# Attention and a two-level mixture of experts on one core: six edits to queues, slots and evictions

## The chip, the cores and the metric

The kernel runs on 1 core of one Trainium2 chip. The metric is device time in microseconds for one execution; the time before is 511.01 us, the median of 3 runs (510.89 to 512.64). The core has TensorE (matrix multiply, PE in the profile, with its weight loads as PEld), VectorE (DVE), ScalarE (ACT), GpSimd (POOL) and the sync engine (SP), which mainly issues transfers. Transfers can be issued on the queues of SP, ACT and GpSimd.

## The reference, cut to what matters

```
def _attn_ref(q, k, v):                      # q: 8 x 16 x 384 x 64, k and v: 8 x 1 x 384 x 64
    scores = 1.0 / np.sqrt(64) * np.matmul(q, k.transpose(0, 1, 3, 2))
    attn = softmax(scores)
    return np.matmul(attn, v)

def _moe_ref(x, w_group, w_expert, w1, w2):  # x: 3072 x 1024, 4 groups of 4 experts, F = 1024
    g_idx = argmax(x @ w_group); g_w = its softmax weight
    for each group g, for its tokens:
        e_idx = argmax(xg @ w_expert[g]); e_w = its softmax weight
        out[token] = g_w * e_w * (np.maximum(xg @ w1[g, e], 0.0) @ w2[g, e])
```

The attention output of each token (16 heads of 64) is the token's x of 1024. Every token goes to one of 16 experts.

## The kernel before, in words

Attention runs batch by batch: 8 batches (b) of 3 row tiles of 128 tokens (t = 3b + j), each tile with 8 units (u) of two heads. The order is written out by hand. The main loop (L782) has 96 slots, 12 for each batch; slot i does units 2i and 2i + 1, four slots make a tile, and p is i mod 4. In each slot TensorE makes the scores (L204) in one of two double banks of PSUM, VectorE takes the row maxima (L215), ScalarE the exponentials with their sums (L218), GpSimd the division (L233), and VectorE transposes the result two slots later into a ring (L239). In slots with p of 2 or 3 TensorE multiplies the tile before with v (pv, L255) into the four rotating banks of `ps_x`, which `xbank` hands out in turn. At p = 3 the result goes to x (`pv_out`, L261), as float32 for the gate and as bf16 (`xb`) for the experts.

The first batch has its own start: `load_k_first` (L134) loads the keys twice, one copy on SP's queue and one on ACT's, then `load_q` (L102) issues the first queries on both queues. TensorE runs 7 matmuls on a blank tile (`busy`, L97), then transposes the keys (`prep_first`, L142), runs 2 more blank ones, and transposes the queries (`q_group`, L172).

The experts of a batch run one batch later. The table `later` holds calls by slot and place in the slot: "s" after the scores, "b" between the two units' softmax, "m0", "m1" and "m2" around the expert's matmuls, "v" before the ring's transposes, "w" after them, "e" after the division, "g" at the end. `advance(n)` (L702) lets the pending expert issue n groups of three steps; its matmuls fill TensorE in slots with p of 0 or 1.

For each batch the gate works on the first tile's tokens (slot 12b + 8: `logits`, L272; slot 12b + 9: `logits_out`, L285, and `gate_first`, L296). `gate_choose` (L336) counts the choices with a matmul on `ones` into a bank of `ps_x`; `gate_score` (L345) reads the bank on VectorE, and `gate_pick` (L353) gives the index of the most chosen expert. That expert, the batch's main one, is applied to the whole batch with the gate as a scale (zero for the other tokens). `load_main` (L457) reads the index into a register on GpSimd and issues the two weight matrices there as four transfers, cast to bf16 on the way, into two buffers for each matrix. `keep_xb` (L467) stores a batch's bf16 x in a scratch tensor on SP's queue; only the loop at the end (L895), for tokens that the main experts did not cover, reads it.

After the main loop comes the end for the last batch, b = 7. `load_second` (L462) loads the second most chosen expert's weights. `few_ready`, `few_turn`, `few_flags`, `few_places` and `few_gather` (L538 to L650) pick out the few tokens of that expert: their x, gate and row number are gathered by matmuls with a selection matrix. `few_gather` moves gate and row number with a float32 matmul (L643). `main_expert(7)` runs meanwhile. Then `few_expert` (L652) applies the second expert to the gathered tokens: hidden layer in two banks (L662), each evicted half by ScalarE and half by VectorE (L670, L672), output in two banks (L678), each again in two halves (L684, L685), and a scatter to the output rows by an indirect transfer on GpSimd (L688). The stores of the main expert (`store`, L532) go out on SP's queue.

Of the kernel before, what the change touches and what calls it, by code (L numbers as in the profile page):

```python
# [11 lines left out]
I32 = mybir.dt.int32  # L12
P = 128
# [6 lines left out]
def kernel(  # L20
# [113 lines left out]
    def load_k_first():  # L134
        kk = qpool.tile([P, NB * D], FP32, tag="kk", bufs=1)
        kk = kk[:, 0:2 * ST * D].rearrange("p (j t d) -> p j t d", j=ST, t=2)
        kv = k[0, 0].rearrange("(p j) d -> p j d", j=ST)
        nc.sync.dma_start(out=kk[:, :, 0, :], in_=kv)
        nc.scalar.dma_start(out=kk[:, :, 1, :], in_=kv)
        st["kk", 0] = kk  # L140
# [397 lines left out]
    def few_ready():  # L538
# [4 lines left out]
        for name, t, widths in (  # L543
            ("16", c16, (("eye", P), ("tri", P), ("sel", ST * P), ("f", 4), ("cum", 4))),
            ("32", c32, (
                ("cols", P), ("tri", P), ("sel", ST * P), ("prod", ST * GE), ("ohs", GE), ("rows", 2 * ST), ("pos", 4),
                ("f", ST), ("fits", 1), ("gate", 1), ("low", 1), ("at", 1),
            )),
        ):
            at_ = 0  # L550
            for part, w in widths:
                fw[part + name] = t[:, at_:at_ + w]
                at_ += w
# [12 lines left out]
        rows = fw["rows32"].rearrange("p (j t) -> p j t", t=2)[:, :, 1]  # L566
# [7 lines left out]
        )  # L574
        fw["xt"] = [ppool.tile([P, Dm], BF16, tag="pr", name="xtok") for _ in range(ST)]
# [48 lines left out]
    def few_gather():  # L624
        fw = st["few"]
        rows = fw["rows32"].rearrange("p (j t) -> p j t", t=2)
        nc.vector.tensor_copy(out=rows[:, :, 0], in_=st["gsel", B - 1][1][:])
# [14 lines left out]
        for j in range(ST):  # L642
            nc.tensor.matmul(  # L643
                out=bank[:, 0:2], lhsT=fw["sel32"][:, ts(j, P)], rhs=rows[:, j, :], start=(j == 0), stop=(j == ST - 1)
            )
        nc.vector.tensor_copy(out=fw["gate32"], in_=bank[:, 0:1])
        nc.vector.tensor_scalar(
            out=fw["at32"].bitcast(I32), in0=bank[:, 1:2], scalar1=fw["fits32"], scalar2=float(NR), op0=ALU.mult,
# [3 lines left out]
    def few_expert():  # L652
# [5 lines left out]
        for half in range(2):  # L658
# [7 lines left out]
            for e in range(2):  # L666
                h = h_t[:, 4 * half + 2 * e:4 * half + 2 * e + 2, 0:P]
                hp = bank[:, ts(e, 2 * P)].rearrange("p (k t) -> p k t", k=2)
                if e:
                    nc.vector.tensor_scalar(out=h, in0=hp, scalar1=0.0, scalar2=None, op0=ALU.max)  # L670
                else:
                    nc.scalar.activation(out=h, in_=hp, func=ACTF.Relu)  # L672
        ys = [bank_end() for _ in range(2)]
        y = pool.tile([P, Dm], FP32, tag="y", name="few_y", bufs=3)
        for part in range(2):
            for nh in range(2):
# [5 lines left out]
                if part:  # L682
                    a, m, z = 512 * nh, 512 * nh + 256, 512 * (nh + 1)
                    nc.scalar.activation(out=y[:, a:m], in_=ys[nh][:, 0:256], func=ACTF.Copy, scale=gate)  # L684
                    nc.vector.tensor_scalar(  # L685
                        out=y[:, m:z], in0=ys[nh][:, 256:512], scalar1=gate, scalar2=None, op0=ALU.mult
                    )
        nc.gpsimd.indirect_dma_start(  # L688
# [34 lines left out]
    for b in range(B):  # L723
        s0 = SB * b
        for x, j0, j1 in ((s0 + 8, 0, 1), (s0 + 16, 1, ST)):
            at(x, "m2", logits, b, j0, j1)
            at(x + 1, "v", logits_out, b, j0, j1)
        at(s0 + 9, "v", gate_first, b)
        at(s0 + 9, "m2", gate_choose, b)
        at(s0 + 9, "w", gate_score, b)  # L730
        at(s0 + 9, "w", gate_pick, b)
        at(s0 + (13 if b == B - 1 else 12), "w", gate_picked, b)
        at(s0 + 9, "g", load_main, b, 0)
        at(s0 + (10 if b == B - 1 else 9), "g", load_main, b, 1)
        at(s0 + 16, "g", keep_xb, b)
# [46 lines left out]
    for i in range(NSL):  # L782
# [8 lines left out]
        if p < 2:  # L791
# [3 lines left out]
            advance(2 if p == 1 and t % ST > 0 else 1)  # L795
# [36 lines left out]
    run(i + 4, "g")  # L832
# [58 lines left out]
    advance(1000)  # L891
    few_expert()
# [53 lines left out]
```

## Time and profile before

| what | value |
|---|---|
| median of 3 runs | 511.01 us (510.89 to 512.64) |
| the profiled execution | 513.33 us |
| its span, first to last instruction | 511.9 us |
| TensorE busy / its weight loads | 486.9 / 262.6 us |
| VectorE / ScalarE / GpSimd busy | 414.0 / 322.3 / 288.4 us |
| mean granted TensorE clock | 0.991 |
| bytes moved by DMA | 84.14 MB, mean 164 GB/s |

The profile is of one execution. Rows in order of time give the start, the duration, the engine (with q for its queue's issue work), the line, the operation, the tiles and the count of merged instructions; in brackets stands the idle time of the engine before it and what ended it. "issue" means that the engine waited for nothing that the profile shows. A row of a line's statistics has the least, median and largest duration in ns and the first and last start in us. A row of transfers has the tiles, the queue, the count, the size of one and the median time from issue to landing.

### The profile page before, as it was taken

The page shows a single profiled execution, that of the slowest core. Times are in us where ns is not written, and L with a number is a line of the kernel's source. Part 1 is how long each engine was busy: PE and PEld are TensorE (multiplying, and loading weights), DVE is VectorE, ACT ScalarE, POOL GpSimd, SP SyncE. Part 2 cuts the span into 40 slices and gives each one's busy share as a digit, 9 for nine tenths or more (in the row PEclk, how much of TensorE's full clock was granted, in tenths as well). Part 3 has the DMA queues.
Part 4 walks back from the last instruction along what each step waited for, and adds up shares of the span by engine and source line. Part 5 has one row for each costly group of instructions (what it writes and reads, how often), then busy time and mean ns, then how long its engine had stood idle before and what let it go on. Part 6 is the DMA issues. An engine that isn't in the chain of part 4 may idle for free. (4 is left out here: it accounts for less than half of the span.)

```text
span 511.9 us, 20030 instructions
## 1 busy us (share of the span) xinstructions
PE 486.9 (95%) x8245; PEld 262.6 (51%) x8262; DVE 414.0 (81%) x739; ACT 322.3 (63%) x1002; POOL 288.4 (56%) x518
## 2 busy tenths in 40 slices
PE   7687799999999999999999999999999999999993
PEld 3144355555465455555465455555455455555651
DVE  3899979988789889998799879988899879871621
ACT  3776766676675775676676776676676766652511
POOL 1656855584576654584576654584576664574200
PEclk9799999999999999999999999999999999999998
DMA  8522898379945999389946999389946992089992
GB/s 109 128 45 43 150 238 213 74 144 232 255 97 106 213 249 229 74 142 231 264 91 113 215 245 226 74 148 232 255 94 120 219 231 96 3 149 246 260 239 86
DMA packets 65180, 84.14 MB, mean 164 GB/s; under 512 B 21163, under 2 KB 40619, under 8 KB 65088
## 3 DMA queue, kind: packets, MB, share of 16 engines
q0 software_dynamic: 19152, 37.84, 40.9%
q1 hardware_dynamic: 44448, 44.65, 35.0%
q8 instruction: 66, 1.08, 0.8%
q10 hardware_dynamic: 1488, 0.36, 0.4%
q14 instruction: 26, 0.21, 0.1%
HBM read 101.61 MB, written 19.40 MB: 236 GB/s over the span
## 5 line engine op out<-in xcount | busy, mean ns | idle before, releaser
L233 POOL TENSOR_SCALAR pr<-pr,rinv 128x384 f32<-128x384 f32 x384 | 218.3, 589 | 153.5 <-DVE rinv L229 140.5
L218 ACT ACTIVATE pr<-s,nmx 128x384 f32<-128x384 f32 x384 | 218.0, 579 | 132.9 <-DVE nmx L215 119.4
L215 DVE TENSOR_REDUCE nmx<-s 128x2 f32<-128x768 f32 x192 | 174.4, 948 | 45.8 <-PE s L204 44.8
L239 DVE STREAM_TRANSPOSE ring<-pr 128x768 f32<-128x768 f32 x192 | 175.2, 951 | 0.0
L204 PE MATMUL s<-kt,qt 64*64 64x384 f32 x1536 | 151.9, 505 | 12.3 <-ACT pr L218 10.2
L255 PE MATMUL x<-ring,v_sb 32*64 32x256 f32 x4608 | 138.1, 378 | 0.2 <-issue 0.2
L255 PEld LDWEIGHTS x<-ring,v_sb 32*64 32x64 f32 x4608 | 101.8, 131 | 43.2 <-issue 23.5
L204 PEld LDWEIGHTS s<-kt,qt 64*64 64x64 f32 x1536 | 48.0, 133 | 83.6 <-ACT pr L218 43.9
L218 ACT ACTIVATION_READ_ACCUMULATOR pr<-s,nmx 128x1 f32 x384 | 77.9, 203 | 0.0
L477 PE MATMUL x<-xb,w 128*128 128x384 bf16 x448 | 76.5, 327 | 0.0
L477 PEld LDWEIGHTS <-w 128*128 128x128 bf16 x512 | 48.2, 98 | 42.6 <-issue 12.6
L491 PE MATMUL x<-w,h_t 128*128 128x512 bf16 x276 | 64.6, 380 | 0.6
L491 PEld LDWEIGHTS <-h_t 128*128 128x128 bf16 x384 | 35.8, 98 | 52.0 <-issue 11.9
L452 POOL DMA_DIRECT2D w<-in_moe_w_dram x36 | 27.9, 784 | 6.0 <-PE sb L491 4.3
L269 ACT COPY xt<-x 128x256 f32<-128x256 f32 x96 | 28.8, 386 | 3.2 <-PE x L255 2.9
L483 ACT ACTIVATE h_t<-x 128x384 bf16<-128x384 f32 x56 | 25.4, 503 | 5.9 <-PE x L477 3.1
L270 POOL CAST xb<-xt 128x1024 bf16<-128x1024 f32 x24 | 25.0, 1040 | 4.6 <-ACT xt L269 4.6
L509 ACT ACTIVATE y<-x,gsel 128x512 f32<-128x512 f32 x36 | 25.0, 693 | 3.3 <-PE x L491 3.3
L193 DVE STREAM_TRANSPOSE qt<-q_sb 128x512 f32<-128x512 f32 x38 | 26.1, 687 | 0.0
L491 PE MATMUL sb<-w,h_t 128*128 128x512 bf16 x92 | 21.2, 379 | 0.2
L509 ACT ACTIVATE y<-sb,gsel 128x512 f32<-128x512 f32 x9 | 6.2, 688 | 16.8 <-PE sb L491 16.8
L229 DVE RECIPROCAL rinv<-ssum 128x4 f32<-128x4 f32 x96 | 13.8, 143 | 3.1 <-ACT pr L218 3.1
(126 smaller groups left out, 168.3 us busy)
## 6 DMA issues: line engine op xcount, KB each, us to landing
w<-in_moe_w_dram POOLq DMA_DIRECT2D x36, 1024.0 KB, 19.7
q_sb<-in_q_dram SPq DMA_DIRECT2D x76, 224.0 KB, 6.3
out_dram<-y SPq DMA_DIRECT2D x96, 128.0 KB, 6.3
xb_scratch<-xb SPq DMA_DIRECT2D x8, 768.0 KB, 4.3
v_sb<-in_v_dram SPq DMA_DIRECT2D x32, 96.0 KB, 3.7
kk<-in_k_dram SPq DMA_DIRECT2D x28, 92.0 KB, 4.2
q_sb<-in_q_dram SPq DMA_DIRECT2D x16, 128.0 KB, 3.4
q_sb<-in_q_dram ACTq DMA_DIRECT2D x4, 64.0 KB, 3.3
```

The source lines that it names most:

```text
L193: nc.vector.transpose(out=qt[:].rearrange("p (x d) -> p x d", d=32), in_=q_sb[:, :, 0:32])
L204: nc.tensor.matmul(out=s[m * D:(m + 1) * D, h, 0:S], lhsT=qt[r, ts(2 * cc + m, D)], rhs=kt[r, :], start=True, stop=True, tile_position=(h ...
L215: nc.vector.tensor_reduce(out=nmx[:], in_=s[:, :, 0:S], axis=AX.X, op=ALU.max, negate=True)
L218: nc.scalar.activation(out=pr[:, h, :], in_=s[:, h, 0:S], func=ACTF.Exp, bias=nmx[:, h:h + 1], scale=1.0, accum_out=ssum[:, k, h:h + 1],)
L233: nc.gpsimd.tensor_scalar(out=pr, in0=pr, scalar1=rinv[:, k, h:h + 1], scalar2=1.0, op0=ALU.mult, op1=ALU.mult)
L239: nc.vector.transpose(out=ring[:, (u // 4) % 3, u % 4].rearrange("p h s -> p (h s)"), in_=st.pop(("pr", u))[:].rearrange("p h s -> p (h s)"),)
L255: nc.tensor.matmul(out=o[i][h * D:(h + 1) * D, 0:2 * P].rearrange("d (g c q) -> d g c q", g=2, c=4), lhsT=v_sb[r, n, :], rhs=ring[r, a:z + ...
L269: nc.scalar.copy(out=xt[:, :, ts(i, 32)], in_=o[:, 0:2 * P].rearrange("p (c q) -> p c q", c=KO))
L452: nc.gpsimd.dma_start(out=w[:, o:o + 4, :], in_=(w1f, w2f)[n][ds(e, 1), :, o:o + 4, :].rearrange("o p c f -> (o p) c f"))
L477: nc.tensor.matmul(out=hp[:, 0:S], lhsT=w1[:, ko, ts(fc, P)], rhs=xb[:, ko, :], start=(ko == 0), stop=(ko == KO - 1))
L491: nc.tensor.matmul(out=yp, lhsT=h_t[:, fo, ts(j, P)], rhs=w2[:, fo, ts(nh, 512)], start=(fo == 0), stop=(fo == FO - 1),)
L509: nc.scalar.activation(out=y[:, ts(nh, 512)], in_=yp, func=ACTF.Copy, scale=g)
```

## The change

Six edits, all in the order of work or in small tiles:

1. The two copies of the first keys are issued on GpSimd's queue, after the identity is made and before `wge` is cleared.
2. Batch 0's count is issued in slot 10, after that slot's scores, its score between the two units' softmax, and the pick and the weights' load at the end of that slot. In the other batches the count stays in slot 12b + 9 but stands one `advance(1)` earlier, at a new place "m3" between the last two groups. The transpose of the first logits and `gate_first` move from "v" to "m0", which leaves VectorE's order as it was.
3. The last batch's main weights are issued at "w", before the slot's division on GpSimd, instead of at "g", behind it.
4. The last batch's bf16 x is kept (`keep_xb`) after the last store of the main expert, instead of before that expert begins.
5. In `few_expert` each bank is evicted by one engine: the first by ScalarE, the second by VectorE.
6. In `few_gather` gate and row number are split into bf16 parts (three and two), moved with a bf16 matmul and added up again.

```diff
@@ load_k_first
-        nc.sync.dma_start(out=kk[:, :, 0, :], in_=kv)
-        nc.scalar.dma_start(out=kk[:, :, 1, :], in_=kv)
+        for t in range(2):
+            nc.gpsimd.dma_start(out=kk[:, :, t, :], in_=kv)
@@ few_ready
-            ("16", c16, (("eye", P), ("tri", P), ("sel", ST * P), ("f", 4), ("cum", 4))),
+            ("16", c16, (("eye", P), ("tri", P), ("sel", ST * P), ("f", 4), ("cum", 4), ("parts", 5 * ST))),
...
+        nc.gpsimd.tensor_copy(out=parts[:, :, 3], in_=rows)
+        nc.gpsimd.tensor_tensor(out=parts[:, :, 4], in0=rows, in1=parts[:, :, 3], op=ALU.subtract)
@@ few_gather
-        rows = fw["rows32"].rearrange("p (j t) -> p j t", t=2)
-        nc.vector.tensor_copy(out=rows[:, :, 0], in_=st["gsel", B - 1][1][:])
+        parts, rest = fw["parts16"].rearrange("p (j t) -> p j t", t=5), fw["rest32"]
+        gsel = st["gsel", B - 1][1][:]
+        nc.vector.tensor_copy(out=parts[:, :, 0], in_=gsel)
+        nc.vector.tensor_tensor(out=rest, in0=gsel, in1=parts[:, :, 0], op=ALU.subtract)
+        nc.vector.tensor_copy(out=parts[:, :, 1], in_=rest)
+        nc.vector.tensor_tensor(out=parts[:, :, 2], in0=rest, in1=parts[:, :, 1], op=ALU.subtract)
...
-                out=bank[:, 0:2], lhsT=fw["sel32"][:, ts(j, P)], rhs=rows[:, j, :], start=(j == 0), stop=(j == ST - 1)
+                out=bank[:, 0:5], lhsT=fw["sel16"][:, ts(j, P)], rhs=parts[:, j, :], start=(j == 0), stop=(j == ST - 1)
             )
-        nc.vector.tensor_copy(out=fw["gate32"], in_=bank[:, 0:1])
+        nc.vector.tensor_reduce(out=fw["gate32"], in_=bank[:, 0:3], axis=AX.X, op=ALU.add)
+        nc.vector.tensor_reduce(out=fw["row32"], in_=bank[:, 3:5], axis=AX.X, op=ALU.add)
@@ few_expert
-            for e in range(2):
...
+            h, hp = h_t[:, 4 * half:4 * half + 4, 0:P], bank.rearrange("p (k t) -> p k t", k=4)
+            if half:
+                nc.vector.tensor_scalar(out=h, in0=hp, scalar1=0.0, scalar2=None, op0=ALU.max)
+            else:
+                nc.scalar.activation(out=h, in_=hp, func=ACTF.Relu)
...
+                if part and nh:
                     nc.vector.tensor_scalar(
-                        out=y[:, m:z], in0=ys[nh][:, 256:512], scalar1=gate, scalar2=None, op0=ALU.mult
+                        out=y[:, ts(nh, 512)], in0=ys[nh], scalar1=gate, scalar2=None, op0=ALU.mult
                     )
+                elif part:
+                    nc.scalar.activation(out=y[:, ts(nh, 512)], in_=ys[nh], func=ACTF.Copy, scale=gate)
@@ the table of calls
-            at(x + 1, "v", logits_out, b, j0, j1)
-        at(s0 + 9, "v", gate_first, b)
-        at(s0 + 9, "m2", gate_choose, b)
-        at(s0 + 9, "w", gate_score, b)
-        at(s0 + 9, "w", gate_pick, b)
+            at(x + 1, "v" if j0 else "m0", logits_out, b, j0, j1)
+        at(s0 + 9, "m0", gate_first, b)
+        at(s0 + (9 if b else 10), "m3" if b else "s", gate_choose, b)
+        at(s0 + (9 if b else 10), "w" if b else "b", gate_score, b)
+        at(s0 + (9 if b else 10), "w", gate_pick, b)
         at(s0 + (13 if b == B - 1 else 12), "w", gate_picked, b)
-        at(s0 + 9, "g", load_main, b, 0)
-        at(s0 + (10 if b == B - 1 else 9), "g", load_main, b, 1)
-        at(s0 + 16, "g", keep_xb, b)
+        if b == B - 1:
+            at(s0 + 9, "w", load_main, b, 0)
+            at(s0 + 10, "w", load_main, b, 1)
+        else:
+            at(s0 + (9 if b else 10), "g", load_main, b, 0)
+            at(s0 + (9 if b else 10), "g", load_main, b, 1)
+            at(s0 + 16, "g", keep_xb, b)
@@ the main loop
-            advance(2 if p == 1 and t % ST > 0 else 1)
+            advance(1)
+            run(i, "m3")
+            if p == 1 and t % ST > 0:
+                advance(1)
@@ the end
-    run(i + 4, "g")
...
     advance(1000)
+    keep_xb(b)
     few_expert()
```

More of the change, by code (lines that the diff above doesn't have):

```diff
@@ L564, in few_ready @@
         nc.gpsimd.memset(c16[:, 2 * P + ST * P:2 * P + ST * P + 8], 0.0)
-        rows = fw["rows32"].rearrange("p (j t) -> p j t", t=2)[:, :, 1]
+        rows, parts = fw["rows32"], fw["parts16"].rearrange("p (j t) -> p j t", t=5)
         nc.gpsimd.iota(
```

13 lines of the change are left out of this document (2 added, 11 removed).

## The prediction

> **What bounds the kernel now.** I read the page's busy shares and slices first, then busy time by stretch, who waited for whom on TensorE, and the order of time at the three places that the change touches.
>
> ```profile
> 300.00:400.00 100.00, 99.79 (x1775) 53.93 (x1764) 88.75 (x152) 68.09 (x218) 63.06 (x110) 1.00 0.79 172
> ```
>
> After the stretch's bounds, the columns are the length, the busy time of TensorE, its weight loads, VectorE, ScalarE and GpSimd (with counts), the granted clock, the DMA share and GB/s. TensorE has no free time here (99.79 of 100 us, clock 1.00), and the same holds from some 60 us to 500 us. Work moved between other engines there is worth nothing; only TensorE work, or a wait of TensorE, is. What remains is the start, batch 0 (no expert work beside it yet), and the last 10 us.
>
> Times add up against the profiled execution (513.33 us, span 511.9, so 1.4 us lie around it). It is 2.3 us above the median 511.01; I carry differences over to the median. The runs shown spread over 1.7 us, so I take 0.5% (2.55 us) as what a measurement of this kernel tells from no change.
>
> **First keys.** The start in order of time, and the landing times:
>
> ```profile
> 1.08 0.68 SPq L138 DMA_DIRECT2D kk<-in_k_dram  x1
> 1.35 0.29 POOL masks.py:199 TENSOR_SCALAR_AFFINE_SELECT ident<-ident 128x128 f32<-128x128 f32 x1
> 3.78 0.15 PEld L100 LDWEIGHTS <-blank 128*128 128x128 bf16 x1 [0.28 <-issue]
> 4.29 0.18 PEld L146 LDWEIGHTS x<-ident,kk 128*128 128x128 f32 x1 [0.36 <-issue]
> 5.06 0.36 PEld L100 LDWEIGHTS <-blank 128*128 128x128 bf16 x2
> 6.09 0.72 PEld L181 LDWEIGHTS x<-ident,q_sb 128*128 128x128 f32 x4 [0.67 <-issue]
> ...
> kk<-in_k_dram SPq DMA_DIRECT2D x1, 96.0 KB, 3.1
> kk<-in_k_dram ACTq DMA_DIRECT2D x1, 96.0 KB, 2.6
> ```
>
> The keys land at 1.08 + 3.1 = 4.18, just as the seven blank matmuls run out (one load each 0.43 us, so the next slot is 4.21), and their transposes begin at 4.29. The two blanks after them would end at 5.06 + 0.86 = 5.92 and the queries' transposes start at 6.09: the keys have 0.17 us of slack, and nothing could start more than that sooner. All later work hangs on this chain.
>
> After the change both halves go out on GpSimd's queue, behind the identity (1.35 + 0.29 = 1.64). SP's and ACT's query issues move up by one key issue (0.68 us); nothing waits for that, because TensorE takes the keys first. What a GpSimd issue costs is seen on the weights only:
>
> ```profile
> 52.22 3.25 POOL L452 DMA_DIRECT2D w<-in_moe_w_dram  x4 [1.64 <-issue]
> L452 POOL DMA_DIRECT2D w<-in_moe_w_dram x36: 750/770/990, 52.2 to 472.0; - x36
> issue: 1.6, 1
> DMA to landing us min/median/max: 8.3/8.3/8.3
> 56.00:57.00 1.00, 1.00 (x15) 0.41 (x4) 0.91 (x2) 0.42 (x2) 1.00 (x3) 1.00 1.10 199
> ```
>
> The first GpSimd issue of the program stood 1.64 us with nothing to wait for and then took 0.99 us; of the other 35 none stood so, and the median is 0.77. I read it as a cost of the first use. The keys become that first use: 1.64 + 1.64 = 3.28, first issue done 4.27, second lands 2.6 us later (ACT's row, the same 96 KB) at 6.87. That is 2.6 us after 4.29, less 0.17 of slack: **+2.4**. Lower end: no first-use cost, 1.64 + 0.77 + 2.6 = 5.0, +0.5; or below it nothing late at all, −0.2 with the slack. Upper end: the first weight half landed 8.3 us after its issue; 1.05 MB at the 199 GB/s of that stretch are 5.3, which leaves 3.0, and 96 KB add 0.5: 4.27 + 3.5 = 7.8, +3.3. I take 2.6 as the landing since its row has the same size. The identity's cover is no help: it ends before either issue could.
>
> The Trainium skill (DMA: Bandwidth & Descriptors, Specifications) puts the first byte at about 1 µs on GpSimd's path and 0.6 µs on SP's and ACT's, which alone would make the keys some 0.4 us later beside the later issue. The rows above carry a larger and one-off delay; the page has none for it, and the sum goes by the rows.
>
> **Batch 0's count.** Slots 9 to 12 in order of time:
>
> ```profile
> 45.66 1.83 DVE L239 STREAM_TRANSPOSE ring<-pr 128x768 f32<-128x768 f32 x2
> 45.79 0.17 PE L339 MATMUL x<-first,ones 128*128 128x16 bf16 x1 [1.81 <-DVE first L304]
> 45.89 0.21 PEld L204 LDWEIGHTS s<-kt,qt 64*64 64x64 f32 x8 [2.08 <-ACT pr L218]
> 47.41 0.14 DVE L348 SCALAR_TENSOR_TENSOR scr<-x,tie 128x16 f32<-128x16 f32 x1
> 47.54 2.41 PEld L255 LDWEIGHTS x<-ring,v_sb 32*64 32x64 f32 x96 [0.70 <-DVE scr L348]
> 48.13 1.79 DVE L215 TENSOR_REDUCE nmx<-s 128x2 f32<-128x768 f32 x2
> 50.44 0.88 PE L204 MATMUL s<-kt,qt 64*64 64x384 f32 x8
> 51.64 1.82 DVE L215 TENSOR_REDUCE nmx<-s 128x2 f32<-128x768 f32 x2
> 55.14 1.52 PE L204 MATMUL s<-kt,qt 64*64 64x384 f32 x16
> 56.09 1.82 DVE L215 TENSOR_REDUCE nmx<-s 128x2 f32<-128x768 f32 x2 [0.82 <-PE s L204]
> ```
>
> The count's 1.81 us stall of TensorE goes: slot 10's scores load some 0.5 us sooner. But VectorE has no gap from 45.66 to 53.4, and its work is only reordered. What is late next is the bank: pv takes four rotating banks, the last of them the count's, so it waits for L348 (0.70 in the row). After the change L348 stands behind slot 10's first reduce: 47.41 + reciprocal 0.1 + reduce 0.91 + 0.14 = 48.6 instead of 47.55. So pv starts 1.06 later, ends at 51.5 (2.85 long), and the next scores, behind it on TensorE, go from 50.44 to 51.5. Their reduce follows 0.95 later (55.14 to 56.09), at 52.45 instead of 51.64: 0.8 later. I take **+0.5**, since slot 10's exponentials, some 0.5 us sooner, can give part of it back. Ends: −0.5 (only the stall counts) and +1.1 (pv's whole delay). Batch 0's weights are issued a step later, some 4 us; the experts need them 20 us after, and the normalisations behind that issue on GpSimd are read two slots later, so both are covered; if not, batch 0's first expert would wait.
>
> For the other batches the count moves up by one eighth of an expert's first half:
>
> ```profile
> 441.33 4.08 PE L477 MATMUL x<-xb,w 128*128 128x384 bf16 x24
> 443.22 0.18 DVE L304 TENSOR_TENSOR first<-oh 128x16 bf16<-128x16 f32 x1
> 445.24 0.17 PE L339 MATMUL x<-first,ones 128*128 128x16 bf16 x1
> 446.41 2.28 POOL L233 TENSOR_SCALAR pr<-pr,rinv 128x384 f32<-128x384 f32 x4 [4.44 <-DVE rinv L229]
> 448.63 1.58 POOL L452 DMA_DIRECT2D w<-in_moe_w_dram  x2
> ```
>
> L339 comes 4.08/3 = 1.36 sooner, at 443.9; its input is ready at 443.4. Covered by 0.5 us, so nothing; were the cover gone, seven batches would pay the lateness. The last batch's weights pass four normalisations, 2.2 us sooner, and these come 1.6 us later, two slots ahead of their readers: nothing.
>
> **The end.**
>
> ```profile
> xb_scratch<-xb SPq DMA_DIRECT2D x1, 768.0 KB, 9.8
> 500.00:501.00 1.00, 0.88 (x5) 0.33 (x4) 0.42 (x1) 0.38 (x1) 0.00 (x0) 1.00 1.09 375
> 502.51 1.89 PE L678 MATMUL sb<-w,few_h 128*128 128x512 bf16 x8 [0.52 <-DMA w<-in_moe_w_dram]
> 504.43 0.47 ACT L684 ACTIVATE few_y<-sb,c 128x256 f32<-128x256 f32 x1 [0.39 <-PE sb L678]
> 504.94 0.48 DVE L685 TENSOR_SCALAR few_y<-sb,c 128x256 f32<-128x256 f32 x1 [0.38 <-ACT few_y L684]
> 505.72 1.12 POOL L688 DMA_INDIRECT out_dram<-few_y,c  x1 [22.35 <-DVE few_y L685]
> 490.40 8.94 SPq L534 DMA_DIRECT2D out_dram<-y  x12
> L511 DVE TENSOR_SCALAR y<-sb,gsel 128x512 f32<-128x512 f32 x3 | 2.3, 751 | 7.7 <-PE sb L491 4.4 <-PE x L879 3.3
> ```
>
> DMA is full to 501, and TensorE waits 0.52 for the last weights. The 768 KB of x leave their way (some 3 us of transfer at about 250 GB/s), and the weights start sooner: the 0.52 goes. The two halves of the last bank ran one behind the other, 504.43 to 505.42 = 0.99; one engine takes 0.75: 0.24 goes. **−0.8**; ends −0.2 (weights still late) and −1.0. On SP x is issued behind the last store, at 499.4; with the landing of 9.8 us it is there by 509.2, about when the scattered rows are, so it costs nothing, or 0.5 if slower. The hidden-layer evictions are merged too, but TensorE reaches their readers later.
>
> ```profile
> 485.19 0.83 PE L643 MATMUL x<-c 128*128 128x2 f32 x6
> 485.88 3.61 PE L491 MATMUL sb<-w,h_t 128*128 128x512 bf16 x15
> ```
>
> Gates in parts: three more small VectorE operations (0.14 for one, by L348's row) make the input ready at 485.19 + 0.45 = 485.6; three single-pass matmuls instead of six passes are done at about 486.0, where L491 began at 485.88: **+0.1** (−0.3 to +0.5). GpSimd's two added operations fall into idle time.
>
> **Sum:** 2.4 + 0.5 − 0.8 + 0.1 = +2.2. 511.01 + 2.2 = **513.2** (profiled: 515.5).
>
> **Rivals.**
>
> 1. *The clock* (slower). TensorE then sits empty from 4.84 until the keys come. After a sparse stretch in the kernel before, the clock fell:
>
> ```profile
> 18.00:19.00 1.00, 1.00 (x12) 0.30 (x8) 0.97 (x3) 0.54 (x2) 0.06 (x1) 0.50 1.03 230
> ```
>
> At 0.50 eight score matmuls take about 1.3 instead of 0.88 us, 0.4 for each of the first three slots: +1.2, 514.4, and up to 515.3 with the late landing (+0.9). For it speaks that the dip is there already; against it that the same dip may only move. It decides once the keys are over 2 us late. The Trainium skill (TensorE: Matmul & The Clock Gate) gives two clocks, half when idle for a window of about 3.4 µs and full after one busy; by that the gap falls short of a window but can spoil the first one.
>
> 2. *No first-use cost*: keys at 5.0, start +0.5 instead of +2.4, so 511.3. For it: the stall is one event. Against: nothing else explains it.
>
> 3. *Everything hides and gains* (faster): start −0.2, batch 0 −0.5, end −1.0, gates −0.3, and the clock dip of 17 to 25 us falls elsewhere, −0.8: −2.8, 508.2. Against it: keys issued later must land as soon.
>
> 4. *The weights are late all the same*, held by their own queue: the end gives −0.2, 513.8.
>
> **How the numbers follow.** Forecast 0.40 (own range 512.2 to 514.2, of it 0.16 above 513.57), rival 1 0.17, rival 2 0.20, rival 3 0.16 (0.01 of it within), rival 4 0.07. Faster 0.15; within 0.5% 0.24 + 0.20 + 0.01 = 0.45; slower 0.16 + 0.17 + 0.07 = 0.40. The range 509.3 to 515.0 leaves out the ends of rivals 3 and 1.
>
> **What would show it.** Keys' transposes at about 6.9, GpSimd idle ahead of its first key issue; L348 behind the first reduce of slot 10 and pv 1 us later; no DMA wait at the last matmuls. Keys before 5 us, or pv no later, would make me wrong.

## The result, and the profile after

The changed kernel took 515.91 us, the median of 6 runs (514.21 to 516.32), beside 511.7 us for the kernel before on the same chip (6 runs, 510.89 to 512.64). The ratio is 1.0077, with a 95% interval of 1.0057 to 1.0097. It is slower, by 4.2 us where 2.2 were forecast, and above the top of the range.

The profiled execution of the changed kernel took 516.11 us (span 514.6), that of the kernel before 513.33 (span 511.9). The two differ by 2.8 us only, because the profiled execution of before was 1.6 us above its median. So the experiments below are compared by medians, and traces by places in the program.

The start of the changed kernel in order of time (columns as before):

```profile
1.84 1.71 POOL L139 DMA_DIRECT2D kk<-in_k_dram  x2 [0.20 <-issue]
7.33 0.50 PEld L146 LDWEIGHTS x<-ident,kk 128*128 128x128 f32 x3 [3.40 <-issue]
7.36 0.88 PE L146 MATMUL x<-ident,kk 128*128 128x128 f32 x3 [2.52 <-DMA kk<-in_k_dram]
9.97 2.84 PE L204 MATMUL s<-kt,qt 64*64 64x384 f32 x16
...
56.37 3.07 POOL L452 DMA_DIRECT2D w<-in_moe_w_dram  x4
...
450.69 0.82 POOL L452 DMA_DIRECT2D w<-in_moe_w_dram  x1 [5.15 <-issue]
```

Its view of transfers has the landing of the keys, in the last column:

```profile
kk<-in_k_dram POOLq DMA_DIRECT2D x2, 96.0 KB, 4.3
```

The issue stands 0.20 us and not 1.64: no first-use cost at this place, and none at batch 0's weights either (56.37 has no idle time in brackets). The last batch's first weights, moved ahead of the division by edit 3, stand 5.15 us with the same mark "issue", so this mark ahead of a weights' issue is not peculiar to a first use; what the engine waits for there stays open. But the keys land 4.3 us after their issue, where ACT's queue took 2.6 and SP's 3.1 for the same 96 KB. The transposes begin at 7.33, 3.04 after the 4.29 of before. The 16 scores of slot 0 then take 2.84 us; before, the same row was

```profile
7.25 1.61 PE L204 MATMUL s<-kt,qt 64*64 64x384 f32 x16
```

Batch 0's count, with the transposes of the ring as a mark:

```profile
48.13 1.83 DVE L239 STREAM_TRANSPOSE ring<-pr 128x768 f32<-128x768 f32 x2
49.91 0.18 PE L339 MATMUL x<-first,ones 128*128 128x16 bf16 x1
50.02 0.67 PE L255 MATMUL x<-ring,v_sb 32*64 32x256 f32 x12
50.78 0.16 DVE L348 SCALAR_TENSOR_TENSOR scr<-x,tie 128x16 f32<-128x16 f32 x1
51.00 2.81 PE L255 MATMUL x<-ring,v_sb 32*64 32x256 f32 x84 [0.30 <-DVE scr L348]
53.73 1.52 PE L204 MATMUL s<-kt,qt 64*64 64x384 f32 x16
```

The mark is 2.47 us later than before (45.66). The first 12 of the 96 pv matmuls now run ahead of the score L348; the other 84 wait for it and go on at 51.00, 3.46 after the start of pv before (47.54). The next scores are 3.29 later (50.44 to 53.73). So most of pv is late by 0.99 beyond what the start had cost, and the scores behind it by 0.82. The count no longer waits.

Then, 40 us later, comes something that the prediction did not have. Slot 19 in the changed kernel, and the same place before:

```profile
88.32 1.52 PE L204 MATMUL s<-kt,qt 64*64 64x384 f32 x16
89.77 1.08 PE L255 MATMUL x<-ring,v_sb 32*64 32x256 f32 x23
92.24 2.39 PE L255 MATMUL x<-ring,v_sb 32*64 32x256 f32 x73 [1.39 <-issue]
94.56 1.52 PE L204 MATMUL s<-kt,qt 64*64 64x384 f32 x16
```

```profile
86.15 1.52 PE L204 MATMUL s<-kt,qt 64*64 64x384 f32 x16
87.60 2.85 PE L255 MATMUL x<-ring,v_sb 32*64 32x256 f32 x96
90.38 1.52 PE L204 MATMUL s<-kt,qt 64*64 64x384 f32 x16
```

The 96 pv matmuls of this slot, 2.78 us from their start to the next scores before, now take 4.79. They stop after the 23rd, and the gap is marked "issue": the profile shows no semaphore, no transfer of data and no other engine that was waited for. That is 2.0 us in one place.

The end of the changed kernel:

```profile
489.11 3.61 PE L491 MATMUL sb<-w,h_t 128*128 128x512 bf16 x15
503.09 3.69 PE L683 MATMUL sb<-w,few_h 128*128 128x512 bf16 x15
506.01 0.69 ACT L692 ACTIVATE few_y<-sb,c 128x512 f32<-128x512 f32 x1 [3.85 <-PE sb L683]
506.88 0.75 DVE L688 TENSOR_SCALAR few_y<-sb,c 128x512 f32<-128x512 f32 x1 [2.90 <-PEq L907]
508.53 1.14 POOL L693 DMA_INDIRECT out_dram<-few_y,c  x1 [21.91 <-DVEq L907]
```

L491 is 3.23 later than before (485.88), as late as the program is by then. The last matmul ends at 506.78 where it ended at 504.40, so 2.38 later: 0.85 was won here, the 0.52 of the DMA wait among it. But the scatter starts 0.90 after the last eviction (507.63 to 508.53), where it started 0.30 after it (505.42 to 505.72), and 2.81 later than before. Of the gain 0.43 went back.

### The profile page after: what moved, and what is told of

Its sections match the earlier page's. It is cut to its first block, busy times and chain, and to the rows that moved or that the text cites. A ratio compares the mean times of both kernels' runs of the same rounds, so it can differ in the third digit from the quotient of the medians.

```text
span 514.6 us, 20025 instructions
## 1 busy us (share of the span) xinstructions
PE 485.7 (94%) x8242; PEld 262.5 (51%) x8259; DVE 414.0 (80%) x741; ACT 321.1 (62%) x1000; POOL 289.4 (56%) x522
## 5 line engine op out<-in xcount | busy, mean ns | idle before, releaser
L204 PE MATMUL s<-kt,qt 64*64 64x384 f32 x1536 | 150.2, 500 | 13.6 <-ACT pr L218 13.1
L204 PEld LDWEIGHTS s<-kt,qt 64*64 64x64 f32 x1536 | 48.5, 133 | 81.8 <-ACT pr L218 42.3
L491 PE MATMUL x<-w,h_t 128*128 128x512 bf16 x276 | 64.6, 380 | 0.6
L491 PEld LDWEIGHTS <-h_t 128*128 128x128 bf16 x384 | 35.7, 98 | 51.9 <-issue 11.9
L491 PE MATMUL sb<-w,h_t 128*128 128x512 bf16 x92 | 21.2, 379 | 0.2
L229 DVE RECIPROCAL rinv<-ssum 128x4 f32<-128x4 f32 x96 | 13.8, 144 | 3.0 <-ACT pr L218 3.0
```

The lines of the kernel that those rows point to most:

```text
L204: nc.tensor.matmul(out=s[m * D:(m + 1) * D, h, 0:S], lhsT=qt[r, ts(2 * cc + m, D)], rhs=kt[r, :], start=True, stop=True, tile_position=(h ...
L491: nc.tensor.matmul(out=yp, lhsT=h_t[:, fo, ts(j, P)], rhs=w2[:, fo, ts(nh, 512)], start=(fo == 0), stop=(fo == FO - 1),)
```

## The experiments

Times are medians beside the kernel before on the same chip. The edits are to the kernel before ("before +") or to the changed kernel ("after").

### Which edits carry the loss

Five kernels: each suspected edit alone, each taken back out of the change, and both taken back.

The first keys on GpSimd's queue, alone:

```diff
-        nc.sync.dma_start(out=kk[:, :, 0, :], in_=kv)
-        nc.scalar.dma_start(out=kk[:, :, 1, :], in_=kv)
+        for t in range(2):
+            nc.gpsimd.dma_start(out=kk[:, :, t, :], in_=kv)
```

> The kernel before with the first keys on GpSimd's queue and nothing else. Theory A (the keys cost the whole path their lateness of some 3 us, and everything behind only moves with them): 3.0 us over before, about 514.7, keys' transposes at 7.3 us, no gap of TensorE in slot 19. Rival B (the keys are nearly all of the 4.2 us, the rest hides): 3.7 us or more over before. Rival C (the keys' lateness is mostly won back by slot 8, as 1.0 of 3.46 us in the two profiles): 2.4 us, 514.1.

The change with this edit undone:

> The changed kernel with the first keys back on SP's and ACT's queues. Theory A: 1.2 us over before (512.9), made of batch 0's later weights (some 2 us in slot 19) and the end's gain. Rival B: level with before or 0.5 us under it (511.2 to 511.7), no gap in slot 19.

Batch 0's count, score, pick and weights in slot 10, alone:

```diff
-        at(s0 + 9, "m2", gate_choose, b)
-        at(s0 + 9, "w", gate_score, b)
-        at(s0 + 9, "w", gate_pick, b)
+        at(s0 + (9 if b else 10), "m2" if b else "s", gate_choose, b)
+        at(s0 + (9 if b else 10), "w" if b else "b", gate_score, b)
+        at(s0 + (9 if b else 10), "w", gate_pick, b)
...
-        at(s0 + 9, "g", load_main, b, 0)
-        at(s0 + (10 if b == B - 1 else 9), "g", load_main, b, 1)
+        at(s0 + (9 if b else 10), "g", load_main, b, 0)
+        at(s0 + (10 if b in (0, B - 1) else 9), "g", load_main, b, 1)
```

> The kernel before with batch 0's count, score, pick and weights in slot 10 and nothing else. Theory A (the later weights keep the DMA engines full while TensorE's next instructions are fetched): 2 us over before, 513.7, with a gap of TensorE in slot 19 put down to issue. Rival B (that gap is a chance of when TensorE's instructions are fetched and hangs on the keys or on nothing): 0.3 us over before, 512.0, no gap in slot 19. My prediction's step (pv waits 1.06 us for the score) would give 0.5 in slots 10 to 12 in either case.

The change with that put back to slot 9:

> The changed kernel with batch 0's count and weights back in slot 9 (the count at its new place between the last two groups). Theory A: 2.0 to 2.3 us under the changed kernel, 513.7, no gap in slot 19. Rival B: 0.3 us under it, 515.6, the gap still there.

And the change with both put back, which leaves the other batches' count, the last weights, x at the end, the evictions and the gates in parts:

> The changed kernel with the first keys and batch 0's count both back; the other batches' count, the last weights, the last x, the evictions by bank and the bf16 parts stay. Theory A (keys 3.2, batch 0's late weights 2.3, the rest gains 1.0 to 1.5): 1.0 to 1.5 us under before, 510.5 to 511.0. Rival B (the parts are not additive, the rest gains nothing by itself): level with before, 511.9.

| kernel | median, us (runs) | kernel before | difference | ratio, 95% interval |
|---|---|---|---|---|
| changed kernel | 515.91 (6) | 511.7 | +4.2 | 1.0057 to 1.0097 |
| before + keys | 515.17 (6) | 511.95 | +3.2 | 1.0051 to 1.0086 |
| after, keys back | 512.78 (12) | 511.95 | +0.8 | 1.0005 to 1.0038 |
| before + batch 0's count and weights | 514.29 (6) | 511.95 | +2.3 | 1.0036 to 1.0076 |
| after, count and weights back | 514.2 (9) | 511.95 | +2.2 | 1.0031 to 1.0069 |
| after, both back | 511.0 (12) | 511.64 | −0.6 | 0.9973 to 0.9998 |

The parts alone give 3.2 + 2.3 − 0.6 = 4.9, and the whole costs 4.2: they add up but for 0.7. Measured from the other side, batch 0's edit costs 1.4 (0.8 + 0.6) on top of the remaining edits, so its size is known to about 1 us. The remaining edits gain about what was forecast for them (−0.8 for the end and +0.1 for the gates). The keys cost 0.8 more than forecast, batch 0 costs 1.8 more; less the 0.7, and with the 0.1 of the rest, these are the 2.0 us between the forecast +2.2 and the measured +4.2.

Four of these five kernels came out near the theory A of their texts, and the last gained 0.6 where 1.0 to 1.5 were expected.

The cleanest pair of traces is the change with both put back beside the change with the keys back, which has batch 0's edit and not the keys. The scores of slot 18 begin at 84.75 and 85.10, 0.35 later; the scores of slot 20, the first row in the one and the second in the other, are 2.00 later:

```profile
89.07 1.52 PE L204 MATMUL s<-kt,qt 64*64 64x384 f32 x16
```

```profile
91.07 1.52 PE L204 MATMUL s<-kt,qt 64*64 64x384 f32 x16
```

Between them lies slot 19 with the gap. The two profiled executions differ by 2.1 us (510.83 and 512.93), so in this pair slot 19 is 1.65 of it. With the count and weights back, no gap was expected there; a smaller one came all the same, at the same matmul:

```profile
89.63 1.94 PEld L255 LDWEIGHTS x<-ring,v_sb 32*64 32x64 f32 x73 [0.58 <-issue]
```

### What in batch 0's edit costs

Only the issue of batch 0's weights a slot later, with the count in its old place:

```diff
-        at(s0 + 9, "g", load_main, b, 0)
-        at(s0 + (10 if b == B - 1 else 9), "g", load_main, b, 1)
+        at(s0 + (9 if b else 10), "g", load_main, b, 0)
+        at(s0 + (10 if b in (0, B - 1) else 9), "g", load_main, b, 1)
```

> The kernel before with batch 0's weights issued a step later, its count left in slot 9. Theory A (the late weights fill the DMA engines when TensorE's instructions of slot 19 are due): 1.5 to 2 us over before, 513.5 to 514, with the gap put down to issue in slot 19's pv. Rival B (the count's new place does it): level with before, no gap there. My prediction had this part at nothing.

513.57 us (12 runs) beside 511.64: +1.9, ratio 1.0018 to 1.0043. So the weights, which the prediction priced at nothing, are nearly all of it, and the count's own move is left with some 0.4 (2.3 − 1.9), about the +0.5 of the forecast. Slot 19 of this kernel, in order of time:

```profile
84.06 1.52 PE L204 MATMUL s<-kt,qt 64*64 64x384 f32 x16
85.51 1.09 PE L255 MATMUL x<-ring,v_sb 32*64 32x256 f32 x23
87.84 2.39 PE L255 MATMUL x<-ring,v_sb 32*64 32x256 f32 x73 [1.25 <-issue]
90.17 1.52 PE L204 MATMUL s<-kt,qt 64*64 64x384 f32 x16
```

The same gap, after the same 23rd matmul, with no other edit in. Batch 0's expert never waited for a weight; what was late was not the weights. This profiled execution (512.14) is the fastest of the twelve and lacks a stall of 0.99 us that the kernel before has in slot 15, so the +1.9 stands on the medians, and its place on the pair of traces above.

The step is also smaller than the 4 us of the prediction. The issues begin at 52.85 here and at 52.22 before, the row maxima of slot 12 at 55.67 and 56.09, so against the program the weights are some 1.1 us later (1.3 in the changed kernel, by 56.37 and 58.90): the 1.64 us that the issue had stood in the kernel before are gone.

A gap at one fixed place of the program with nothing to wait for points at the instructions. The view of transfers has a queue for them, in the changed kernel as in the kernel before:

```profile
q8 instruction: 66, 1.08, 0.8%
```

The columns are packets, MB and the share of 16 engines' span. q8 has 66 packets of 16.4 KB; divided by the 8242 matmuls and 8259 weight loads of the page this is one packet for 250 TensorE instructions and 65 bytes for one. I read it as TensorE's own program, fetched in blocks while it runs. If such a block is late, TensorE stops where the block before it ends.

The places of the stalls agree with that. The changed kernel stalls in slot 15 too (until 71.04, 0.44 us, "issue"). From there to the end of slot 19's gap TensorE runs 380 matmuls and 379 weight loads, in the columns of the view by stretch:

```profile
71.03:92.23 21.20, 19.52 (x380) 10.81 (x379) 19.60 (x33) 14.40 (x48) 12.47 (x25) 1.00 1.03 234
```

That is 759, three blocks of 253.

### Full queues, late weights, or the two together

My first theory was that the block of slot 19 is late since the queues are still full then. The copy of batch 0's x to DRAM (768 KB, slot 16) stands in the same stretch. So I moved it away, with the weights late:

```diff
-        at(s0 + 16, "g", keep_xb, b)
+        at(s0 + (16 if b else 22), "g", keep_xb, b)
```

> The kernel before, with batch 0's weights issued in slot 10 and the copy of x to DRAM for batch 0 moved from slot 16 to slot 22. Theory A: TensorE stalls in slot 19 because its instructions are fetched by the same DMA queues, which are full until about 90 us; without the copy's 768 KB in that stretch they are empty some 3 us sooner, the stall in slot 19 vanishes, and the time is within 0.5 us of the kernel before (511.3 to 512.2). Theory B: the stall hangs on something else than the full queues (the program's place, the order of issues): it stays, 1.9 us over the kernel before (513.3 to 514).

512.58 us (12 runs) beside 512.05, +0.5 with a ratio of 0.9997 to 1.002; expected were 512.2 at most by the first theory, 513.3 at least by the second, and the weights alone had cost 1.9. The place in order of time:

```profile
87.21 3.35 PE L255 MATMUL x<-ring,v_sb 32*64 32x256 f32 x96
88.17 1.94 PEld L255 LDWEIGHTS x<-ring,v_sb 32*64 32x64 f32 x73 [0.33 <-issue]
90.49 1.52 PE L204 MATMUL s<-kt,qt 64*64 64x384 f32 x16
```

Of the gap 0.5 us is left (3.35 instead of 2.85). That fits full queues, though the change with both put back and one output engine (below) shows 3.35 here as well, with the weights in their old place. The counter-test is to leave the weights in their old place and fill the queues with a second copy of x:

```diff
+        if b == 0:
+            nc.sync.dma_start(out=xb_dram[B], in_=st["xb", b][:].rearrange("p c t -> p (c t)"))
```

> The kernel before, with everything in its old place and one more transfer: batch 0's x (768 KB) is stored a second time, into a spare row of the scratch tensor, right behind the first store in slot 16. Theory A: the stall of TensorE in slot 19 comes when the DMA queues are still full as it gets there, whatever fills them; 768 KB more at about 250 GB/s keep them full some 3 us longer, to about 89 us, so the stall appears with the weights in their old place: a gap of about 1.1 us among the pv matmuls of slot 19, and about +1.9 us over the kernel before (513.2 to 514.0). Theory B: it takes the later issue of the weights: no gap, and the time within 0.5 us of the kernel before.

512.05 us (12 runs) beside 512.2, ratio 0.9984 to 1.0012: no cost, and the pv matmuls of slot 19 run through:

```profile
86.96 2.89 PE L255 MATMUL x<-ring,v_sb 32*64 32x256 f32 x96
89.78 1.52 PE L204 MATMUL s<-kt,qt 64*64 64x384 f32 x16
```

So full queues alone do not make the long stall, and my first theory falls. The test was weaker than planned: the second copy kept the queues full to about 87 us and not to 89 (DMA share 0.96 from 86 to 87 us, 0.32 from 87 to 88). But the kernel with count and weights late has much the same shares there (0.94 and 0.28), and the gap.

What sets the kernels with the long gap apart is how much of the weights is still to be moved as the copy is issued. What each queue moved in the 10 us from the copy's issue (76.39, 75.75 and 78.55), in the kernel before, with the second copy, and in the changed kernel; q0 moves the weights (GpSimd's queue), q1 what SP and ACT issue:

```profile
q0 software_dynamic: 277, 0.53, 28.5%
```

```profile
q0 software_dynamic: 188, 0.35, 18.8%
```

```profile
q0 software_dynamic: 412, 0.81, 43.0%
```

With the weights alone late it is 0.95 MB. So the weights overlap the copy in the kernel before too, and more of them where they are late: 0.80 to 0.95 MB in the four kernels with the long gap, at most 0.54 in the others that have the copy there. When the block begins, from the view of transfers in windows of 0.1 us, against the scores of slot 18 as a mark of how far TensorE is:

| kernel | weights late | copy in slot 16 | block begins | scores of slot 18 | block after the mark | pv goes on at |
|---|---|---|---|---|---|---|
| before | no | yes | 85.2 | 86.15 | −0.9 | no gap |
| before + second copy | no | twice | 84.7 | 85.51 | −0.8 | no gap |
| after, both back | no | yes | 84.0 | 84.75 | −0.7 | no gap |
| after, both back, one output engine | no | yes | 83.4 | 83.86 | −0.4 | 86.28 |
| after, count and weights back | no | yes | 86.8 | 86.97 | −0.1 | 89.63 |
| before + weights, copy in slot 22 | yes | no | 85.6 | 85.76 | −0.2 | 88.17 |
| changed, copy in slot 22 | yes | no | 88.4 | 89.86 | −1.5 | no gap |
| after, keys back | yes | yes | 85.8 | 85.10 | +0.7 | 88.75 |
| before + weights late | yes | yes | 85.1 | 84.06 | +1.0 | 87.84 |
| before + count and weights | yes | yes | 85.9 | 84.92 | +1.0 | 88.57 |
| changed kernel | yes | yes | 89.3 | 88.32 | +1.0 | 92.24 |

With a gap, TensorE goes on 2.6 to 3.0 us after the block began. Without one, the 24th pv matmul is due 0.7 after the slot's first, at 88.3 before and 87.7 with the second copy, 3.1 and 3.0 after the block: just in time. So slot 19 had hardly any slack to begin with. In the four kernels with the weights late and the copy in slot 16 the block comes 1.6 to 1.9 us later against the program than in the kernel before, and only they have a gap of over 1 us. Two kernels with the weights in their old place have a block up to 0.8 later, and a smaller gap (0.33 and 0.58): the block's lateness varies without these edits too, by causes that these runs do not show. Whether a late block waits behind the packets of the weights and the copy in an engine's queue, or behind something else that all three need, is not shown either.

The last run asks whether this is what the changed kernel itself loses: all six edits, and batch 0's copy in slot 22.

> The changed kernel, with the copy of x to DRAM for batch 0 in slot 22 instead of slot 16 and all else as changed. Theory A: the stall of slot 19 needs the weights' transfers and the copy in the queues together when TensorE's next instructions are asked for; without the copy there the pv matmuls of slot 19 run through in about 2.8 us (4.79 from their start to the next scores in the changed kernel) and the time is about 1.9 us under the changed kernel's 515.9, so 513.6 to 514.6. Theory B: with all six edits in, the keys' lateness moves that place so that it is late all the same: the gap stays, and the time is within 0.5 us of 515.9.

514.66 us (11 runs) beside 512.04, ratio 1.003 to 1.0066, so +2.6 where the changed kernel had +4.2. The place in order of time:

```profile
89.86 1.52 PE L204 MATMUL s<-kt,qt 64*64 64x384 f32 x16
91.31 2.85 PE L255 MATMUL x<-ring,v_sb 32*64 32x256 f32 x96
94.09 1.52 PE L204 MATMUL s<-kt,qt 64*64 64x384 f32 x16
```

No gap, 2.78 from pv to the scores as before. The gain is 1.25 us by the medians, just short of what was expected (1.3 to 2.3), and 1.6 by the differences to the kernel before. In part the gap is missing because TensorE comes later: it reaches the scores of slot 18 at 89.86, 1.54 after the changed kernel, while the block begins at 88.4, only 0.9 before the changed kernel's. At the changed kernel's pace some 0.5 to 0.9 us of gap would have been left (an estimate: the block and 2.6 to 3.0 us, against the 24th matmul due at 90.5), if the block had not moved with TensorE. A stall of the same kind, in slot 15, was longer in this profile (1.28 us) than in the changed kernel's (0.44): the blocks' lateness varies, and with it a part of the gain.

### What in the keys costs

Three theories for the landing of 4.3 us. First, other transfers at the start are in the way: tile 1's queries are issued only after the values.

> The kernel before with the first keys on GpSimd's queue and the queries of tile 1 issued after the gate's weights and v, so that few transfers share the DMA engines with the keys. Only the start is looked at (the queries of tile 1 come late, so the whole is longer). Theory A (the keys are late because their packets share the engines with the queries'): the landing falls from 4.3 us towards 2.6 to 3.1, transposes at 6 us or sooner. Rival B (the landing on GpSimd's path is long by itself): landing still over 4 us, transposes at 7 us or later.

One run, 514.96 us. The landing is 4.1 to 4.4 us and the transposes begin at 7.31, no sooner than with the keys alone (7.18): contention with these queries is not it. Tile 0's queries, which go out beside the keys, were left where they are, so they stay a possible cause.

Second, the issue: the keys go out ahead of the identity.

> The kernel before, with the first keys on GpSimd's queue but issued ahead of the identity that GpSimd writes. Theory A: the landing of 4.2 to 4.4 us is fixed to this path and no first-use stall stands at the start, so only the issue moves, from 1.84 to about 1.1 us: the transposes begin at about 6.5 (7.3 in the kernel before with the keys on GpSimd), and the time is about +2.4 us over the kernel before (513.9 to 514.3). Theory B: the first DMA of GpSimd waits for something that is only ready at about 3 us, so an earlier issue lands no earlier: transposes at 7.3, +3.2 us (about 515).

515.94 us (4 runs) beside 512.05, ratio 1.0044 to 1.0094: nothing won. In order of time, where L74 is the new place of the keys' issue and L145 their transposes:

```profile
1.65 1.71 POOL L74 DMA_DIRECT2D kk<-in_k_dram  x2 [0.87 <-POOLq L929]
7.41 0.59 PE L145 MATMUL x<-ident,kk 128*128 128x128 f32 x3 [2.77 <-DMA kk<-in_k_dram]
```

The issue came only 0.19 us sooner, because it stood 0.87 at GpSimd's queue, and the landing took 4.6. The keys were there no sooner, as theory B has it; since the issue did not move to 1.1, the run does not tell a fixed landing from something that is ready only at about 3 us.

Third, what the pause does to TensorE: 16 blank matmuls at the start instead of 7.

```diff
-    busy(7)
+    busy(16)
```

> The kernel before, with the first keys on GpSimd's queue and 16 blank matmul groups at the start where it has 7, so that TensorE is busy until the keys land. Theory A: of the +3.2 us that the keys cost, about 1.2 is the lower clock after a pause of TensorE (the 16 scores of slot 0 took 2.84 us where they took 1.61): with the blanks they take about 1.6 again and the time is about +2.0 us over the kernel before (513.5 to 514.0). Theory B: the scores' 2.84 us hide behind ScalarE's exponentials, or the clock is low for another reason: no gain, +3.2 us (about 515).

514.8 us (4 runs) beside 512.05, +2.75, ratio 1.0039 to 1.0074. The start in order of time:

```profile
1.67 5.13 PE L100 MATMUL x<-blank 128*128 128x512 bf16 x16 [1.67 <-DVE blank L74]
...
4.63 1.67 PEld L100 LDWEIGHTS <-blank 128*128 128x128 bf16 x8 [0.28 <-issue]
...
7.25 0.52 PE L146 MATMUL x<-ident,kk 128*128 128x128 f32 x3 [0.45 <-DMA kk<-in_k_dram]
8.88 1.52 PE L204 MATMUL s<-kt,qt 64*64 64x384 f32 x16 [0.24 <-ACT qt L185]
```

The blank matmuls come every 0.43 us until 4.63 and then every 0.21: here TensorE doubles its pace after 3.0 us of work. With seven blanks it is at 4.84 just there and then pauses for 2.5 us. With sixteen, the transposes take 0.52 instead of 0.88 and the scores 1.52 instead of 2.84, and slot 0's reciprocal (L229) comes at 13.21 us, where it came at 14.99 with the keys alone and at 11.67 before. So of 3.3 us at this place 1.8 are the pace after the pause in this pair of traces, and 1.5 the lateness of the keys.

The size varies. All six traces with the keys late and seven blanks have slow scores in slot 0 (2.19 to 2.84 us), and their reciprocal comes at 13.96 to 15.13, which is 0.75 to 1.9 us behind the 13.21 of the run with sixteen. The transposes right behind the pause are slow in two of the six (0.88) and fast in four (0.52 to 0.59). Nor does the granted clock (the column ahead of the last two) always show it: in the changed kernel it reads 1.00 where the slow scores run, and with the count and weights back 0.50:

```profile
9.00:11.00 2.00, 1.97 (x13) 1.09 (x15) 0.00 (x0) 0.74 (x2) 0.00 (x0) 1.00 0.85 24
```

```profile
8.50:11.00 2.50, 2.47 (x18) 0.80 (x16) 0.58 (x1) 0.62 (x2) 0.00 (x0) 0.50 0.93 40
```

The Trainium skill (TensorE: Matmul & The Clock Gate, What's actually happening) puts the change of pace at about 3.4 µs of sustained work; the trace shows 3.0 here, and slow work again after a pause of 2.5.

The whole time fell by less. The lead of this profiled run over that of the keys alone was 1.8 us in slot 14, 0.1 in slot 17 and 0.95 in the last slots: at the end of slot 14 it had a stall "issue" of 1.4 us, where the other had one of 0.48 a little later. The interval of the time, 514.05 to 515.84 us, leaves out theory A's 513.5 to 514.0; with 4 runs the 0.45 between the two differences (2.75 and 3.2) settles no more than that. The pace after the pause is seen in the rows at the start; that it costs the whole time as much is not shown.

### The end

The change without keys and batch 0's edit still starts its scatter late. In it, and then with both output banks evicted by VectorE:

```profile
501.55 0.75 DVE L688 TENSOR_SCALAR few_y<-sb,c 128x512 f32<-128x512 f32 x1 [2.90 <-PEq L907]
503.19 1.12 POOL L693 DMA_INDIRECT out_dram<-few_y,c  x1 [21.92 <-DVEq L907]
```

```diff
-                if part and nh:
+                if part:
                     nc.vector.tensor_scalar(
...
-                elif part:
-                    nc.scalar.activation(out=y[:, ts(nh, 512)], in_=ys[nh], func=ACTF.Copy, scale=gate)
```

> As the run with both parts back, but both output banks of the few tokens evicted by VectorE, so that the scatter waits for one engine only. Theory A (the scatter, which waits for ScalarE and VectorE, starts 0.9 us after the last eviction instead of 0.3): the scatter follows 0.3 us after the last eviction, 0.6 us under the other run, 1.6 to 2 us under before, 510.1. Rival (the 0.6 us come from the stores or from x on their way): the gap stays 0.9 us, level with the other run.

```profile
499.70 1.55 DVE L688 TENSOR_SCALAR few_y<-sb,c 128x512 f32<-128x512 f32 x2 [2.04 <-PE sb L683]
501.55 1.12 POOL L691 DMA_INDIRECT out_dram<-few_y,c  x1 [21.27 <-DVEq L905]
```

From the last eviction's end to the scatter it is 0.30 us with one engine (501.25 to 501.55) and 0.89 with two (502.30 to 503.19). The time is 510.84 us (12 runs) beside 511.64, ratio 0.9962 to 0.9989: faster than both kernels, by 0.8 us against the kernel before, where 1.6 to 2 were expected. Against its neighbour with two engines (511.0) the 0.16 is too small to tell, so the 0.6 us are shown in the rows and not in the time.

The number of engines alone does not decide. In the kernel before, the two halves of the last bank also came from two engines, and the scatter started 0.30 after the last. There VectorE's half had waited for ScalarE's (504.94, "[0.38 <-ACT few_y L684]" in the prediction's row), so I read it that a wait for VectorE's covered both; in the changed kernel VectorE's eviction waits for TensorE and not for ScalarE (506.88), and the scatter starts 0.90 after it. All traces with the evictions of before have 0.30 or 0.31, all with those of the changed kernel 0.89 or 0.90.

## Why the prediction was wrong, and where it was right

**The step that failed** is the sentence that batch 0's weights, issued a step later, "both are covered", since the experts need them 20 us after. They were covered: no wait for weights appeared, and batch 0's expert was not late. But the cover was checked against the readers of the weights only. The same 4 MB, 1.1 to 1.3 us later against the program and not 4, reached further into the copy of x, and what came late behind the two was a block of TensorE's instructions. This term stood at 0 and measured +1.9 (weights alone) of the +2.3 of batch 0's edit. It was outside the ends −0.5 and +1.1, because no row was looked for that would price a later transfer for those who share its queues. The view of TensorE's waits before had the row: the stall of slot 15 ("PE s L204 <- issue: 1.0" among TensorE's waits) reads as the same thing, three blocks earlier, and it was left out of the prediction.

**The keys** had the right sign and place, and a wrong make-up. Of the +2.4, the 1.64 of first use did not come (0.20), and the landing, taken as 2.6 from ACT's row, was 4.3: transposes at 7.33 instead of 6.9. The slack of 0.17 was about right: the transposes are 3.04 late (4.29 to 7.33) and the scores 2.72 (7.25 to 9.97), so 0.3 was hidden. Behind it came what rival 1 describes: with the keys over 2 us late the scores of slot 0 run at a slow pace. Rival 1 put 0.4 on each of the first three slots; 0.75 to 1.9 up to slot 0's reciprocal was measured. In sum +3.2, inside the bounds −0.2 to +3.3 but at their end. Rival 2 was right that there is no first use, and wrong about the time, since it kept the short landing.

**Batch 0's count** itself behaved nearly as worked out: no wait at the count, pv 0.99 late (1.06 forecast, though the first 12 matmuls of pv do not wait), the scores behind it 0.82 (0.8), some +0.4 in the end (+0.5).

**The end** won 0.85 up to the last matmul, with the 0.52 of the wait for weights gone as said; rival 4 did not come. One engine per bank was priced at its eviction alone (−0.24). It came to −0.17 (1.02 from the last matmul to the last eviction's end before, 0.85 after), and the wait behind it changed: the scatter then has two evictions to wait for, neither of which waited for the other, and starts 0.6 us later. Net −0.42 in the trace instead of −0.8. **Gates in parts** and the other batches' count: L491 begins 2.04 us after the gather's first matmul (487.07 to 489.11) and began 2.06 after it before (483.82 to 485.88), so +0.0 instead of +0.1. With both large edits out, the remainder is −0.6 in medians, −0.7 by the sum.

## What to carry to other kernels

A transfer that moves is priced twice: once for its reader, and once for all that shares its stretch, TensorE's own instruction blocks among it; a gap marked "issue" at a fixed place of the program, where transfers pile up, is the sign, and pulling two large transfers apart shortened or removed it here. What the first matmuls wait for belongs on the queue whose landing the trace shows for that size, since late data slowed TensorE's first scores as well. Where one instruction waits for several producers, an edit to them is priced at that wait and not at the producers alone.

## What the runs showed of the hardware that was not expected

- TensorE's program comes, as I read the rows, in blocks of 16.4 KB for about 250 instructions, over the transfer engines. Where more of the 4 MB of weights lay under a 768 KB copy (0.81 MB after its issue instead of 0.53), a block came 1.6 to 1.9 us later and TensorE stood 1.1 to 1.4 us with no other cause that the profile shows; under a doubled copy with the weights in their old place it did not.
- A 96 KB load of the first keys landed after 4.1 to 4.7 us from GpSimd's queue in seven traces, and after 2.5 to 2.6 from ACT's and 3.0 to 3.3 from SP's in the others. The Trainium skill (DMA: Bandwidth & Descriptors, Specifications) has the first byte after about 1 µs on GpSimd's path and 0.6 µs on the other two; by that 0.4 us of it would be the path (an estimate), and the medians here differ by 0.8 us at least, so part of it is something else.
- The 1.64 us that GpSimd's first issue stood in the kernel before are no cost of first use. They did not move to the keys when these became the first, and with batch 0's weights late and nothing else they are gone as well, as the first weights' row of that kernel shows (no idle time in brackets):

```profile
52.85 3.24 POOL L452 DMA_DIRECT2D w<-in_moe_w_dram  x4
```

- An indirect transfer started 0.9 us after the last of two evictions on two engines that had not waited for each other, and 0.3 us after it where one engine did both or where the later had waited for the earlier.
